# An S4 convolution with a parallel feed-forward block: tiles 0 and 1 loaded and normalised one by one, first weights requested before tiles 2 and 3, the second weight buffer taken into use later

## The chip, the cores and the metric

The kernel runs on one core of one Trainium2 chip. The metric is the device time of one execution in microseconds (us), as the median of several runs. All arithmetic is fp32, or fp32r for the products of TensorE: an operand is split into a high part and the remainder, and three of the four partial products are summed.

## The reference

```python
def reference(A_u, A_A_re, ..., B_x, B_w1, B_w2):
    x = A_u                                   # 1 x 2048 x 576
    xn = layernorm(x)                         # over the 576 columns
    return x + ssm(xn, ...) + ffn(xn, B_w1, B_w2)

def ssm(u, A_re, A_im, B_re, B_im, C_re, C_im, log_dt, Dskip):
    dt = exp(log_dt)                          # 576 channels, 128 states each
    P = exp(dt * A * arange(L))
    K = einsum("dn,dnl,dn->dl", C, P, dt * B).real
    return causal_convolution(u, K) + u * Dskip       # by FFT in the reference

def ffn(x, w1, w2):                           # 576 -> 4608 -> 576
    return silu(x @ w1) @ w2
```

## The kernel before

**Tiling.** The 2048 rows are 16 tiles of 128 rows, handled in pairs. `phase0` takes a pair: it loads it (`load_x`), normalises it (`norm`), transposes each tile on TensorE and splits it into high and low parts (`put_xt`: `xh` by a copy on ScalarE, `xl` by a subtraction on VectorE, and the 64 columns left over in `x4`), and stores the normalised rows to DRAM (`dxn`) for the convolution. Tiles 0 to 3 form block 0 of the feed-forward part and tiles 4 to 7 block 1. Tiles 8 to 15 are transposed in the same way, but their transposes go to DRAM (`dxt`) for the second half.

**The feed-forward part** (`ffn`) runs over two halves of the rows, in each over 36 groups of 128 hidden columns, four groups to a chunk (in the second half, from the third chunk on, in a form with fewer products, `wino_ffn`). For every chunk and block, `up` makes four groups of hidden values (14 products each, into one of two PSUM banks) and the gate (`gf` by SiLU on ScalarE, `gh` a copy, `gl` a subtraction on VectorE). `down` multiplies them with the second weights into `po` and adds the result to `acc` on VectorE. For the very first block, `up` runs in two parts: columns 0 to 255 (tiles 0 and 1) for all four groups, then columns 256 to 511 (tiles 2 and 3).

**Weights.** `load_w1(half, c, t)` loads two groups of first weights at once, as 512, 64 and 64 rows in three DMAs. `split_w1` makes `w1h` (ScalarE, line 266) and `w1l` (VectorE, line 268) of it. There is one raw buffer for them in the pool `wp`; once the pool `w1x` exists, the groups with t = 2 take a second buffer there, and `next_w1` loads a chunk ahead. Second weights are loaded by `load_w2` and split by `split_w2` in the same way (lines 275, 284, 286).

**Beside it** runs `side()`, a generator that `weave` advances at fixed steps of the feed-forward generator: the rest of `phase0`, the parameters of the state-space part (`natural`, whose tables are loaded by SP into memory that the pool `pa` of the first tiles held, lines 652 and 665), the convolution kernel (`kgen`), the spectral product and the tail. The pool `w1x` opens together with `kgen`.

**What sets the order.** The program is written in this woven order. A scheduler then orders the instructions of each engine by its own estimate of time, within the dependences. `tc.issue_after` (in `behind`) keeps instructions behind a named one, `tc.high_priority` moves some ahead. On the chip each engine, and each queue of DMA issues (SP, ScalarE, GpSimd), takes its instructions in that order. The start before is: `side` up to tiles 0 to 3 (`next(sd)`), then the first weights, their splits and the second weights (`next(fg)`), then tiles 4 to 7 (`next(sd)`), then the weave.

Lines that the change and the prediction touch: 118 to 128 (`put_xt`), 161 to 167 (`load_x`), 176 to 197 (`norm`), 199 to 227 (`phase0`, `normed`), 237 to 247 (`load_w1`), 258 to 269 (`split_w1`), 346 to 354 (first loads), 1025 to 1057 (`side`), 1074 to 1079 (start of the program).

Of the kernel before, what the change touches and what calls it, by code (L numbers as in the profile page):

```python
# [41 lines left out]
def kernel(  # L42
# [21 lines left out]
    nc = tc.nc  # L64
    FT = 4
# [44 lines left out]
    acc = {}  # L110
# [4 lines left out]
        x4 = xtp.tile([P, 512], F32R, tag="x4", name=f"x4_{blk}")  # L115
        return xh, xl, x4

    def put_xt(xh, xl, x4, src):

        pt = pss.tile([P, NKT, P], F32, tag="pss", name="pt")  # L120
        for kt in range(NKT):
            nc.tensor.transpose(pt[:, kt, :], src[:, kt * P:(kt + 1) * P], ident)
        nc.scalar.copy(xh, pt)  # L123
        nc.vector.tensor_sub(xl, pt, xh)
        pt = pss.tile([P, 512], F32, tag="pss", name="pt4")
        nc.tensor.transpose(pt[:64, :P], src[:, NKT * P:D], ident)
        pins["xt_s"] = nc.scalar.copy(x4[:64, :], pt[:64, :P]).ins
        pins["xt_v"] = nc.vector.tensor_sub(x4[64:, :], pt[:64, :P], x4[:64, :]).ins
# [32 lines left out]
    def load_x(j, pool, tag, engines):  # L161

        t = pool.tile([P, 2, D], F32, tag=tag, name=f"{tag}{j}")
        for ps, v, eng in quarters(xv, engines):
            eng.dma_start(t[ps], v[:, j:j + 2])
        pairs[j] = t
        return t[:, 0, :], t[:, 1, :]

# [5 lines left out]
    def norm(p0, js, xs):  # L174

        n = len(js)
        st = p0.tile([P, 2, 2, 6], F32, tag="st", name="st")
        mv = p0.tile([P, 2, 2], F32, tag="mv", name="mv")
        for i in range(n):
            for h in range(2):  # L180
                nc.vector.bn_stats(out=st[:, i, h, :], in_=xs[i][:, h * HD:(h + 1) * HD])
            nc.vector.bn_aggr(out=mv[:, i, :], in_=st[:, i, :, :])
        sd = p0.tile([P, 2], F32, tag="sd", name="sd")
        mb = p0.tile([P, 2], F32, tag="mb", name="mb")
        nc.vector.tensor_scalar(sd[:, :n], mv[:, :n, 1], 1e-5, None, op0=ALU.add)
        pins["sd"] = nc.gpsimd.tensor_tensor(sd[:, :n], sd[:, :n], mhalf[:, :n], op=ALU.pow).ins
        xn = p0.tile([P, 2, D], F32, tag="xn", name="xn") if js[0] < 8 else pairs[js[0]]
        for i, j in enumerate(js):
            if j % 2 == 0:
                pins["xn"] = nc.vector.tensor_scalar(xn[:, i, :], xs[i], mv[:, i, 0:1], sd[:, i:i + 1],  # L190
                                                 op0=ALU.subtract, op1=ALU.mult).ins
            else:
                nc.vector.scalar_tensor_tensor(mb[:, i:i + 1], mv[:, i, 0:1], -1.0, sd[:, i:i + 1],
                                               op0=ALU.mult, op1=ALU.mult)
                nc.scalar.activation(xn[:, i, :], xs[i], AF.Identity,
                                     scale=sd[:, i:i + 1], bias=mb[:, i:i + 1])
        return xn

    def phase0(p0, js):
        j0 = js[0]  # L200
        if j0 < 8:
            xs = load_x(j0, accp, "acc", (nc.sync, nc.scalar) if j0 < 4 else (nc.sync,))
            acc.update(zip(js, xs))
        else:
            xs = load_x(j0, p0, "xj", (nc.sync,))
        if j0:
            normed(p0, js, xs)
        else:
            for j, xj in zip(js, xs):
                normed(p0, (j,), (xj,))  # L210

    def normed(p0, js, xs):
        xn = norm(p0, js, xs)
        for i, j in enumerate(js):
            b, jj = divmod(j, 4)
            if b < 2:
                if jj == 0:
                    xts[b] = new_xt(b)
                c = slice(jj * P, (jj + 1) * P)
                xh, xl, x4 = xts[b]  # L220
                put_xt(xh[:, :, c], xl[:, :, c], x4[:, c], xn[:, i, :])
            else:
                xt = p0.tile([P, 9, P], F32R, tag="xt", name="xt", bufs=1)
                put_xt(xt[:, 0:4, :], xt[:, 4:8, :], xt[:, 8, :], xn[:, i, :])
                nc.gpsimd.dma_start(dxt[b - 2][:, :, jj * P:(jj + 1) * P], xt.bitcast(F32))
        eng = nc.sync if js[0] < 8 else nc.gpsimd
        eng.dma_start(dxn[:, js[0]:js[0] + len(js)], xn[:, :len(js)])

    def ffn():
        w2v = w2.rearrange("(t p) d -> p t d", p=P)  # L230
# [6 lines left out]
        def load_w1(half, c, t, pool=None):  # L237

            f = c * FT + t
            first = half == 0 and c == 0  # L240
            r1 = (pool or (pa if first and t else w1x if t and w1x else wp)).tile([P, 5, 2 * P], F32, tag="w1r", name="w1r", bufs=1)
            fs = slice(f * P, (f + 2) * P)
            eng = nc.gpsimd if first and t == 0 else nc.sync
            eng.dma_start(r1[:, 0:4, :], w1[0:512, fs].rearrange("(k p) f -> p k f", p=P))
# [13 lines left out]
        def split_w1(half, c, t):  # L258
            first = half == 0 and c == 0
            r1 = R1.pop((half, c, t))  # L260
            for i in range(2):
                h1 = wp.tile([P, 5, P], F32R, tag="w1h", name="w1h", bufs=FT + 1)
                l1 = wp.tile([P, 5, P], F32R, tag="w1l", name="w1l", bufs=FT + 1)
                src = r1[:, :, i * P:(i + 1) * P]
                with behind(pins.get("gh", pins["xt1s"] if t else None)):
                    nc.scalar.copy(h1, src)
                with behind(pins["xt1"] if first else None):
                    pins["w1l"] = nc.vector.tensor_sub(l1, src, h1).ins
                W1[half, c, t + i] = h1, l1
# [75 lines left out]

        for t in (0, 2):
            load_w1(0, 0, t)
        for t in (0, 2):
            split_w1(0, 0, t)
        for t in range(FT):  # L350
            load_w2(0, 0, t)
        for t in range(FT):
            split_w2(0, 0, t)
        yield 0
# [667 lines left out]
    def side():  # L1022
# [3 lines left out]
        with tc.tile_pool(name="pa", bufs=4) as pa:  # L1026
            for js in ((0, 1), (2, 3), (4, 5), (6, 7)):
                with behind(pins["xt3"] if js[0] > 2 else None):
                    phase0(pa, js)
                pins[f"xt{js[1]}"], pins[f"xt{js[1]}s"] = pins["xt_v"], pins["xt_s"]  # L1030
                if js[0] == 2:
                    yield 0
# [1 line left out]
        with tc.tile_pool(name="kf", bufs=1) as kfp:  # L1034
            for n in ("f", "rho", "phi"):
                kf[n] = kfp.tile([P, D], F32, name=n + "T")
            with tc.tile_pool(name="nat", bufs=1) as nat, tc.tile_pool(name="pb", bufs=2) as pb:
                nt = natural(nat)
                tiles = iter(range(8, NJ, 2))
                for at, tables in ((0.0, 1), (0.02, 0), (0.035, 0), (gate_of(1), 1), (0.06, 0), (gate_of(2), 1), (0.08, 0), (0.085, 1)):  # L1040
# [3 lines left out]
                    else:  # L1044
                        j = next(tiles)
                        with behind(pins["gl"]):
                            phase0(pb, (j, j + 1))
            with behind(pins["sd"]):
                nc.gpsimd.dma_start(f1, cf1)
            nc.sync.dma_start(vt, cv)  # L1050
            with tc.tile_pool(name="up", bufs=1) as up, tc.tile_pool(name="w1x", bufs=1) as w1x:
                sp = spread(up)
                for n, at in enumerate(kgen()):
                    if n > 1:
                        next(sp, None)
                    yield marks[0] + at * (marks[1] - marks[0])
                for _ in sp:
# [13 lines left out]
        yp = ctx.enter_context(tc.tile_pool(name="yp", bufs=3))  # L1071
        yield from tail()

    sd = side()
    next(sd)
    fg = ffn()
    next(fg)
    next(sd)
    weave(fg, 276, sd)
    for j in range(8, 14, 2):  # L1080
        store(pairs[j], j, (nc.sync, nc.scalar))
# [80 lines left out]
```

## Time and profile before

| | us |
|---|---|
| median of 3 runs | 1121.45 |
| lowest and highest | 1119.86, 1123.09 |
| the profiled execution | 1121.59 |
| its span in the trace | 1119.7 |
| TensorE busy | 1091.6 |
| first TensorE instruction | 8.82 |
| first product of the feed-forward part | 12.50 |

The profile is one execution. "L298" is line 298 of the kernel; PE is TensorE's matmul, PEld its weight load, DVE VectorE, ACT ScalarE, POOL GpSimd, SP the engine that issues most DMAs; SPq, ACTq and POOLq are the queues of DMA issues. Matmuls overlap in their pipeline, so the pace of products is read from start to start and not from the length of a row. A window's row gives, for each engine, busy time and number of instructions, then the clock granted to TensorE, the busy share of the DMA engines and GB/s.

### The profile page before, as it was taken

The page shows a single profiled execution, that of the slowest core. Times are in us where ns is not written, and L with a number is a line of the kernel's source. Part 1 is how long each engine was busy: PE and PEld are TensorE (multiplying, and loading weights), DVE is VectorE, ACT ScalarE, POOL GpSimd, SP SyncE. Part 2 cuts the span into 40 slices and gives each one's busy share as a digit, 9 for nine tenths or more (in the row PEclk, how much of TensorE's full clock was granted, in tenths as well). Part 3 has the DMA queues.
Part 4 walks back from the last instruction along what each step waited for, and adds up shares of the span by engine and source line. Part 5 has one row for each costly group of instructions (what it writes and reads, how often), then busy time and mean ns, then how long its engine had stood idle before and what let it go on. Part 6 is the DMA issues. An engine that isn't in the chain of part 4 may idle for free.

```text
span 1119.7 us, 23109 instructions
## 1 busy us (share of the span) xinstructions
PE 1091.6 (97%) x9101; PEld 987.6 (88%) x9101; DVE 950.0 (85%) x1615; ACT 728.1 (65%) x1285; POOL 140.5 (13%) x244
## 2 busy tenths in 40 slices
PE   6998999999999999999999999999999999999998
PEld 5997989889988899898899988899989998999787
DVE  6698899999999999999999978988878888886333
ACT  4665455776777766676667645877767877785330
POOL 1022100000000000000330001112212112111220
PEclk9999999999999999999999999999999999999999
DMA  9455632436353536356964235456455565543985
GB/s 272 141 156 177 194 124 82 144 85 176 105 154 128 150 108 172 120 138 236 237 190 92 72 65 183 133 175 178 140 165 178 163 187 157 167 157 116 247 200 139
DMA packets 161870, 173.68 MB, mean 155 GB/s; under 512 B 88497, under 2 KB 127425, under 8 KB 161121
## 3 DMA queue, kind: packets, MB, share of 16 engines
q1 hardware_dynamic: 137200, 106.75, 34.5%
q0 software_dynamic: 23888, 63.67, 19.2%
q10 hardware_dynamic: 672, 1.77, 0.7%
q8 instruction: 72, 1.18, 0.4%
q14 instruction: 38, 0.30, 0.1%
HBM read 109.64 MB, written 62.60 MB: 154 GB/s over the span
## 4 chain that ended last, share of the span: by engine, by line
PE 70%; DVE 10%; DMA 9%; ACT 5%; issue 4%; SPq 1%; POOL 1%; ACTq 0%; DVEq 0%; POOLq 0%
PE po L328 30%; PE ph L298 16%; PE pb L453 5%; PE kp L866 3%; DMA w<-dw 2%; PE pc L453 2%; DMA w1r<-in_B_w_dram 2%; PE pb L994 2%; PE pu L994 2%; PE pk L994 2%; PE ph L299 1%; PE ph L300 1%; PE z L881 1%; PE pa L453 1%; DMA w2r<-in_B_w_dram 1%
## 5 line engine op out<-in xcount | busy, mean ns | idle before, releaser
L328 PE MATMUL po<-w,gh 128*128 128x288 f32 x2304 | 475.1, 297 | 6.2 <-ACT w L284 2.1
L328 PEld LDWEIGHTS po<-w,gh 128*128 128x128 f32 x2304 | 376.5, 188 | 22.1 <-DMA w<-dw 2.7
L328 PE MATMUL po<-w,gl 128*128 128x288 f32 x1152 | 334.9, 296 | 0.6 <-DVE gl L308 0.6
L328 PEld LDWEIGHTS po<-w,gl 128*128 128x128 f32 x1152 | 215.2, 188 | 2.6 <-DVE gl L308 0.9
L333 DVE TENSOR_TENSOR acc<-po,acc 128x288 f32<-128x288 f32 x296 | 130.3, 452 | 59.7 <-PE po L328 58.6
L298 PE MATMUL ph<-xh,w1h 128*128 128x512 f32 (+1 forms) x368 | 99.1, 388 | 0.9 <-ACT xh L123 0.7
L298 PE MATMUL ph<-xl,w1h 128*128 128x512 f32 (+1 forms) x368 | 98.5, 386 | 0.0
L298 PE MATMUL ph<-xh,w1l 128*128 128x512 f32 (+1 forms) x368 | 97.9, 383 | 0.0
L306 ACT ACTIVATE gf<-ph 128x512 f32<-128x512 f32 (+1 forms) x92 | 53.3, 579 | 60.4 <-PE ph L300 41.8
L298 PEld LDWEIGHTS ph<-xl,w1h 128*128 128x128 f32 x368 | 67.6, 191 | 12.8
L298 PEld LDWEIGHTS ph<-xh,w1l 128*128 128x128 f32 x368 | 66.6, 189 | 11.7
L298 PEld LDWEIGHTS ph<-xh,w1h 128*128 128x128 f32 x368 | 65.2, 191 | 11.2 <-ACT xh L123 1.0
L157 POOL DMA_DIRECT2D d1u<-u x32 | 17.5, 547 | 405.8 <-ACT u L156 404.5
L825 ACT ACTIVATE c<-th,magic 128x1040 f32<-128x1040 f32 x36 | 42.0, 1168 | 40.2 <-DVE C L846 28.0
L307 ACT CAST gh<-gf 128x512 fp32r<-128x512 f32 (+1 forms) x92 | 55.3, 602 | 15.5 <-PE po L328 14.5
L903 POOL DMA_DIRECT2D m<-in_cm_dram x64 | 33.9, 531 | 250.8 <-PE pu L994 147.1
L308 DVE TENSOR_TENSOR gl<-gf,gh 128x512 fp32r<-128x512 f32 (+1 forms) x92 | 60.7, 662 | 3.5 <-ACT gh L307 3.3
L827 ACT ACTIVATE c<-th 128x1040 f32<-128x1040 f32 x36 | 38.7, 1076 | 33.7 <-DVE th L826 33.6
L845 DVE TENSOR_TENSOR S<-th,C 128x1024 f32<-128x1024 f32 x36 | 44.0, 1222 | 12.1 <-ACT th L828 12.0
L470 DVE TENSOR_TENSOR gl<-gf,gh 128x512 fp32r<-128x512 f32 x56 | 38.0, 688 | 11.9 <-ACT gh L469 11.6
L370 ACT CAST w1h<-w1r 128x512 fp32r<-128x512 f32 (+2 forms) x56 | 34.6, 621 | 20.3 <-DMA w1r<-in_B_w_dram 14.6
L826 DVE SCALAR_TENSOR_TENSOR th<-c,th 128x1040 f32<-128x1040 f32 x36 | 44.5, 1237 | 0.7 <-ACT c L825 0.5
(271 smaller groups left out, 2384.5 us busy)
## 6 DMA issues: line engine op xcount, KB each, us to landing
w1r<-in_B_w_dram SPq DMA_DIRECT2D x35, 512.0 KB, 4.2
dw<-w SPq DMA_DIRECT2D x28, 576.0 KB, 4.5
w<-dw POOLq DMA_DIRECT2D x28, 576.0 KB, 6.6
w2r<-in_B_w_dram SPq DMA_DIRECT2D x44, 288.0 KB, 5.0
d1u<-u POOLq DMA_DIRECT2D x32, 288.0 KB, 2.7
d1k<-stage SPq DMA_DIRECT2D x18, 512.0 KB, 7.3
ur<-d1u SPq DMA_DIRECT2D x32, 288.0 KB, 3.3
kr<-d1k SPq DMA_DIRECT2D x32, 288.0 KB, 2.8
```

The source lines that it names most:

```text
L298: nc.tensor.matmul(ph, w[:, kt, :], v[:, kt, a:e], start=n + kt == 0, stop=False)
L306: nc.scalar.activation(gf, ph, AF.Silu)
L307: pins["gh"] = nc.scalar.copy(gh, gf).ins
L308: pins["gl"] = nc.vector.tensor_sub(gl, gf, gh).ins
L328: pins["pe"] = nc.tensor.matmul(po[:, :HD], gs[g][:, js], ws[:, w, hs], start=n == 0 and j not in begun, stop=n == 3 * len(terms) - 1, ski ...
L333: nc.vector.tensor_add(acc[j][:, hs], po[:, :HD], acc[j][:, hs])
L453: pins["pe"] = nc.tensor.matmul(dst, a[:, kt], v[:, kt], start=start and n == 0, stop=stop and n == 5, skip_group_check=True).ins
L825: nc.scalar.activation(c65, th, AF.Identity, bias=magic)
L826: nc.vector.scalar_tensor_tensor(th, c65, MAGIC, th, op0=ALU.subtract, op1=ALU.subtract)
L827: nc.scalar.activation(c65, th, AF.Abs)
L845: nc.vector.tensor_mul(ov3, t[:, :, 0:64].rearrange("n d (x y) -> n d x y", y=32), mv3)
L994: nc.tensor.matmul(dst, st, mv[:, hs], start=n == 0, stop=n == 3 * len(terms) - 1)
```

## The change

- `load_x` loads tiles 0 and 1 as two loads of four DMAs each (72 KB a DMA), first all of tile 0. The pair of tiles 2 and 3, and all later ones, go through SP alone; before, tiles 2 and 3 used SP and ScalarE.
- `phase0` became a generator that stops after the load of tiles 0 to 7. The start steps `side` and `ffn` in turn: load of tiles 0 and 1; first weights' load; tiles 0 and 1 normalised and transposed, load of tiles 2 and 3; second weights' load and first weights' split; tiles 2 and 3; second weights' split; tiles 4 to 7; the weave.
- All first weights are loaded through SP; before, the very first piece went through GpSimd. The normalised rows of tiles 0 to 7 are stored through GpSimd; before, through SP.
- Tile 1 is normalised on VectorE (one `tensor_scalar`), as tile 0 is; before, on ScalarE.
- Tiles 2 and 3 are normalised behind tile 1's last VectorE step. Tile 0's low part waits until both tiles are normalised.
- Of the first four weight copies to `w1h`, the first waits for tile 0's last ScalarE step and the other three for tile 1's; before, the first two waited for no such step.
- The pool `w1x` still opens with `kgen`, but is put to use only from the third step of `kgen`, so the second buffer and the loads a chunk ahead begin later.

Its description also names idle products, products made only to keep TensorE busy: neither the kernel before nor the diff has any.

```diff
-    def put_xt(xh, xl, x4, src):
+    def put_xt(xh, xl, x4, src, low=None):
...
-        nc.vector.tensor_sub(xl, pt, xh)
+        with behind(low):
+            nc.vector.tensor_sub(xl, pt, xh)
...
-        for ps, v, eng in quarters(xv, engines):
-            eng.dma_start(t[ps], v[:, j:j + 2])
+        for i in range(j, j + 2, 1 if j == 0 else 2):
+            for ps, v, eng in quarters(xv, engines):
+                if j == 0:
+                    eng.dma_start(t[ps, i], v[:, i])
+                else:
+                    eng.dma_start(t[ps], v[:, j:j + 2])
...
-            if j % 2 == 0:
+            if j % 2 == 0 or n == 1:
...
     def phase0(p0, js):
         j0 = js[0]
         if j0 < 8:
-            xs = load_x(j0, accp, "acc", (nc.sync, nc.scalar) if j0 < 4 else (nc.sync,))
+            xs = load_x(j0, accp, "acc", (nc.sync, nc.scalar) if j0 == 0 else (nc.sync,))
             acc.update(zip(js, xs))
+            yield
         else:
             xs = load_x(j0, p0, "xj", (nc.sync,))
         if j0:
-            normed(p0, js, xs)
+            with behind(pins["xt1"] if j0 == 2 else None):
+                normed(p0, js, xs)
         else:
-            for j, xj in zip(js, xs):
-                normed(p0, (j,), (xj,))
+            xn = [norm(p0, (j,), (xj,)) for j, xj in zip(js, xs)]
+            last = pins["xn"]
+            for j in js:
+                turned(p0, (j,), xn[j], None if j else last)
+                pins[f"xt{j}s"] = pins["xt_s"]
+
     def normed(p0, js, xs):
-        xn = norm(p0, js, xs)
+        turned(p0, js, norm(p0, js, xs))
+
+    def turned(p0, js, xn, low=None):
...
-        eng = nc.sync if js[0] < 8 else nc.gpsimd
-        eng.dma_start(dxn[:, js[0]:js[0] + len(js)], xn[:, :len(js)])
+        nc.gpsimd.dma_start(dxn[:, js[0]:js[0] + len(js)], xn[:, :len(js)])
...
-            eng = nc.gpsimd if first and t == 0 else nc.sync
+            eng = nc.sync
...
-                with behind(pins.get("gh", pins["xt1s"] if t else None)):
+                with behind(pins.get("gh", pins["xt1s" if t + i else "xt0s"])):
...
         for t in (0, 2):
             load_w1(0, 0, t)
+        yield 0
+        for t in range(FT):
+            load_w2(0, 0, t)
         for t in (0, 2):
             split_w1(0, 0, t)
-        for t in range(FT):
-            load_w2(0, 0, t)
+        yield 0
...
-                    phase0(pa, js)
+                    for _ in phase0(pa, js):
+                        if js[0] <= 2:
+                            yield 0
...
-            with tc.tile_pool(name="up", bufs=1) as up, tc.tile_pool(name="w1x", bufs=1) as w1x:
+            with tc.tile_pool(name="up", bufs=1) as up, tc.tile_pool(name="w1x", bufs=1) as more:
                 sp = spread(up)
                 for n, at in enumerate(kgen()):
                     if n > 1:
+                        w1x = more
                         next(sp, None)
...
-    sd = side()
-    next(sd)
-    fg = ffn()
-    next(fg)
-    next(sd)
+    sd, fg = side(), ffn()
+    for g in (sd, fg, sd, fg, sd, fg, sd):
+        next(g)
     weave(fg, 276, sd)
```

More of the change, by code (lines that the diff above doesn't have):

```diff
@@ L220, in normed @@
                 xh, xl, x4 = xts[b]
-                put_xt(xh[:, :, c], xl[:, :, c], x4[:, c], xn[:, i, :])
+                put_xt(xh[:, :, c], xl[:, :, c], x4[:, c], xn[:, i, :], low)
             else:
@@ L1046, in side @@
                         with behind(pins["gl"]):
-                            phase0(pb, (j, j + 1))
+                            for _ in phase0(pb, (j, j + 1)):
+                                pass
             with behind(pins["sd"]):
```

## The prediction

> **What bounds the kernel now.** I read the page's busy shares, then the table of windows, then the table of waits. Columns of the windows: length, busy time and number of instructions for PE, weight load, VectorE, ScalarE, GpSimd, then granted clock, DMA share, GB/s.
>
> ```profile
> span 1119.7 us, 23109 instructions
> PE 1091.6 (97%) x9101; PEld 987.6 (88%) x9101; DVE 950.0 (85%) x1615; ACT 728.1 (65%) x1285; POOL 140.5 (13%) x244
> ...
> 0.00:12.50 12.50, 2.67 (x11) 1.73 (x11) 5.61 (x22) 4.88 (x9) 4.39 (x11) 1.00 0.89 227
> ...
> 50.00:100.00 50.00, 47.91 (x279) 42.19 (x278) 46.95 (x89) 34.45 (x49) 8.85 (x9) 1.00 0.51 148
> ...
> 400.00:500.00 100.00, 100.00 (x1025) 90.65 (x1015) 97.28 (x147) 69.34 (x105) 4.32 (x8) 1.00 0.43 118
> ```
>
> TensorE sets the time: in the middle it never rests. Only the first 12.5 us (2.67 busy) and the stretch from 50 to 100 (47.91 of 50) leave something to win. The waits say the same:
>
> ```profile
> PE pt L122 <- DVE xn L190: 8.8, 1, 8.8
> PE po L328 <- ACT w L284: 2.1, 1, 2.1
> PE pt L122 <- ACT xj L195: 1.7, 1, 1.7
> ```
>
> All three lie within the first 103 us, where the change works. The amount of products is unchanged, so the new time is the old one minus the idle TensorE time that is really removed. What counts is the lead (how much earlier TensorE stands at the same amount of work) and whether later waits take it back.
>
> **The start.** In order of time, with start, length, engine; a bracket is the idle time before.
>
> ```profile
> 0.74 3.47 DMA acc<-in_A_u_dram
> ...
> 0.74 1.78 SPq L165 DMA_DIRECT2D acc<-in_A_u_dram  x4
> 1.96 0.81 POOL L244 DMA_DIRECT2D w1r<-in_B_w_dram  x1
> 5.66 1.54 DVE L181 BATCH_NORM_STATS2 st<-acc 128x6 f32<-128x288 f32 x4 [4.72 <-DMA acc<-in_A_u_dram]
> 7.11 0.33 DVE L182 BATCH_NORM_AGGREGATE mv<-st 128x2 f32<-128x12 f32 x2
> 7.58 1.22 POOL L186 TENSOR_TENSOR sd<-sd,mhalf 128x1 f32<-128x1 f32 x2 [3.75 <-DVE sd L185]
> 8.18 0.58 DVE L190 TENSOR_SCALAR xn<-acc,mv,sd 128x576 f32<-128x576 f32 x1 [0.55 <-POOL sd L186]
> 8.82 1.12 PE L122 MATMUL pt<-ident,xn 128*128 128x128 f32 x4 [8.82 <-DVE xn L190]
> 9.16 1.54 DVE L181 BATCH_NORM_STATS2 st<-acc 128x6 f32<-128x288 f32 x4 [0.17 <-DMA acc<-in_A_u_dram]
> 10.61 1.35 ACT L266 CAST w1h<-w1r 128x640 fp32r<-128x640 f32 x2
> 11.87 0.58 ACT L123 CAST xh<-pt 128x512 fp32r<-128x512 f32 x1
> 12.35 0.26 ACT L127 CAST x<-pt 64x128 fp32r<-64x128 f32 x1
> 12.50 2.08 PE L298 MATMUL ph<-xh,w1h 128*128 128x256 f32 x8 [0.66 <-ACT xh L123]
> 14.40 3.03 DVE L268 TENSOR_TENSOR w1l<-w1r,w1h 128x640 fp32r<-128x640 f32 x4
> 15.29 2.06 PE L298 MATMUL ph<-xl,w1h 128*128 128x256 f32 x8
> 17.15 0.77 PE L298 MATMUL ph<-xh,w1l 128*128 128x256 f32 x4
> 20.93 0.64 PE L298 MATMUL ph<-xh,w1h 128*128 128x256 f32 x4
> 21.41 0.64 PE L298 MATMUL ph<-xl,w1h 128*128 128x256 f32 x4
> 22.61 0.56 PE L328 MATMUL po<-w,gh 128*128 128x288 f32 x3
> ```
>
> The reader should see a chain, load, statistics, power, normalise, transpose, cast, that ends in the first product at 12.50. Also that eight products from 15.29 to 17.15 take 0.23 each and four from 20.93 take 0.12 each, though the clock column shows 1.00: the first products run at half pace.
>
> **First product.** The whole pair waited for 5.66; its first DMA had landed at 0.74 + 3.47 = 4.21. Tile 0 alone is half the pair and goes first, so I take 4.4. Two statistics (0.77), an aggregate (0.2) and the epsilon (0.2) end at 5.6, the power (0.7) at 6.3. In the changed order tile 1's two statistics stand ahead of tile 0's normalisation on VectorE; tile 1 lands at about 5.7 (as the pair did), so that is free at 6.5 and normalises until 7.1. Transposes at half pace 1.1, to 8.3. ScalarE then does tile 0's casts (0.58 + 0.26, to 9.1), and next in its queue stands the first weight cast, ahead of tile 1's. Tile 1 is normalised at 8.7 on VectorE (ScalarE no longer does it), transposed by 9.85, cast by 10.5. First product 10.5 instead of 12.5: 2.0 gained. The weight cast between them is covered if its load lands by 9.1. It moves from GpSimd's queue to SP's, where it waits for a free DMA slot at about 4.2; the landing row quoted below (3.0/4.9/8.1) gives 9.1 as the middle and 12.3 as the late end. With 12.3, tile 1's cast ends at 13.7 and 1.2 is lost. I take the middle.
>
> **Half of it is given back at tiles 2 and 3.** Before, their statistics ran at 9.16. Now their load stands behind both weight pieces: 0.59 MB for tiles 0 and 1, 0.07 identity, 1.31 weights, 0.59 for tiles 2 and 3 is 2.56 MB, at 0.23 MB/us (first window) 11.1 us after the first packets at 2, so 13.1. VectorE holds these statistics between the second and the third weight subtraction, so the last two (0.76 each) end at 14.7 + 1.5 = 16.3. The first four half groups (56 products) need about 9 us from 10.5, five of them at half pace: 19.4. Tiles 2 and 3 then need, one after the other in ScalarE's order, a normalisation (to 19.7), a gate activation, xh (to 20.7), a gate copy (0.4), x, and xh of tile 3 (0.58): 21.9. Before, all this work of TensorE was behind it at 22.61. The lead is 0.7.
>
> Then the changed order helps: the second four half groups (56 × 0.12 = 6.7) all stand ahead of the second layer's products, so VectorE's statistics of tiles 4 to 7 and the w2 subtractions hide under them. From 21.9 TensorE should run without a wait. Before, it lost another 1.1 until 41 (0.63 of it waiting for gl). Lead at 41: **1.8**. Bounds: 3.2, if ScalarE's chain is not last and work alone sets it; -0.5, if the 0.59 MB of dxn writes, now on GpSimd's queue, get ahead of tiles 2 and 3 (0.59 / 0.23 = 2.5 later).
>
> **The natural loads.**
>
> ```profile
> 40.55 0.27 PE L126 MATMUL pt<-ident,xn 128*64 128x128 f32 x1
> ...
> 40.90 0.33 SPq L665 DMA_DIRECT2D dt<-in_A_log_dt_dram  x1
> 43.16 6.61 DMA cr<-in_A_C_re_dram
> 49.86 0.95 DVE pr L706
> 138.68 0.43 PE L328 MATMUL po<-w,gh 128*128 128x288 f32 x2
> 138.95 0.29 PE L328 MATMUL po<-w,gl 128*128 128x288 f32 x1
> ```
>
> SP's loads of the SSM parameters wait for the last transpose of tile 7, because they reuse its pool. In the changed program 89 second-layer products stand ahead of that transpose, before it was 62: 27 × 0.27 / 2 = 3.6 us more work. So the loads start at 40.9 - 1.8 + 3.6 = 42.7, 1.8 later, and the VectorE chain from 49.86 with them. The queue behind on SP (w2 of the next chunk) moves too, with no use before 70.
>
> **The waits at 94 and 102.**
>
> ```profile
> 86.72 0.59 ACT L123 CAST xt<-pt 128x512 fp32r<-128x512 f32 x1 [6.18 <-DMA dxt<-xt]
> 96.91 0.67 PE L328 MATMUL po<-w,gh 128*128 128x288 f32 x3 [2.09 <-ACT w L284]
> 102.51 0.66 PE L122 MATMUL pt<-ident,xj 128*128 128x128 f32 x4 [1.74 <-ACT xj L195]
> ```
>
> Before, 2.09 + 1.74 and some 0.4 around them are lost, 4.2 in all. In the new order some 6 us more products stand ahead of the fourth w2 tile and of tile 13's transposes, and the fourth w2 load no longer waits behind the third xt cast (the 6.18 row). Both waits should go. Two others come: tile 8's normalisation, 1.8 late on VectorE, against TensorE 1.8 early and with about 2 of slack before (1.6), and the last gate group, whose PSUM bank is freed by an activation that now stands behind the arctangent tables (1.9). Net 4.2 - 3.5 = **0.7** gained. Bounds: 4.2 (none of the new waits) and -1.8 (old waits plus the late loads).
>
> **The second weight buffer.**
>
> ```profile
> DMA to landing us min/median/max: 3.0/4.9/8.1
> ...
> 121.39 0.38 SPq L244 DMA_DIRECT2D w1r<-in_B_w_dram  x1
> 134.63 0.38 SPq L244 DMA_DIRECT2D w1r<-in_B_w_dram  x1
> 140.66 1.20 PE L298 MATMUL ph<-xh,w1h 128*128 128x512 f32 x4 [0.22 <-ACT w1h L266]
> ```
>
> Before, the second half of the third chunk took the extra buffer, whose memory came free late, and TensorE waited 0.4 in all around 140. Now it follows in the one buffer, as soon as the first half is split (119.83 + 1.5 in the old run, by the row order the same place): asked at 121, there at 126, wanted by TensorE 10 us of products earlier than before, at about 127. I take **0.4** gained; the late landing (8.1 instead of 4.9) would cost 3.2 instead. This also bounds what SP's order does to the loads behind it.
>
> Sum: 1.8 + 0.7 + 0.4 = 2.9. The profiled execution took 1121.59 (span 1119.7 and 1.9 around it), 0.14 above the median of the runs shown, so 1121.45 - 2.9 = **1118.6**. The removed ScalarE normalisations, the extra yields, the dxn stores on GpSimd (0.55 each, whose queue idles 3.75 at a time) and the behind-pins cost nothing that I can place: they hide under TensorE, and uncovered the three stores would be 1.7. There are no idle products in the old code to remove.
>
> **The rivals.**
> - *All of it is kept.* The start gives 3.2 and the new waits at 94 to 103 do not come (4.2): 1121.45 - 3.2 - 4.2 + some 0.4 of reordering = 1114. For it: the new order has 6 us more cover there. Against: VectorE is full from 50 to 100 (46.95 of 50).
> - *The lead is given back.* The two new waits were priced with the natural chain 1.8 late. If it comes another 2.5 later (the range of one w1 landing, 4.9 to 8.1, would do it), they grow from 3.5 to 6.0 and eat the 1.8 and the 4.2: 1121. For it: VectorE has no slack to catch up. Against: the old waits hung on ScalarE and a load, not on VectorE.
> - *Slower.* The one buffer for the first weights makes a chain out of split, load and cast. It decides as soon as load and cast need more than the 10 us of products between the two halves of the third chunk. With the late landing the second half costs 3.2, and the next piece, which waits for that split in turn, the same again: 6.4, against the 2.5 gained before: 1121.45 + 3.9 = 1125.4. For it: SP's queue is in order, so what stands ahead delays the load. Against: the fourth chunk is wanted some 40 us later.
> - *The half pace lasts longer.* The start now has gaps between 8 and 11 and again at 20 to 22. If the slow pace holds for 56 more products, 56 × 0.11 = 6.2 less the 3.5 of waits it hides: 1118.6 + 2.7 = 1121.3. [...]
>
> **How the numbers follow.** Forecast 0.40 (its own range 1115 to 1121), all kept 0.22, given back 0.15, slower 0.15, half pace 0.08. A measurement of this kernel can tell about 0.3%, 3.4 us, from no change: under 1118.1 lie all of the second and nearly half of the first, 0.42; over 1124.8 the slower case and a little, 0.17; between, 0.41. The rest of the program is reordered too, which I give 2 us either way. Range 1112 to 1126.
>
> **What would show it.** First product at 10.5 (wrong: after 12). The 256-wide products restart after tile 3's cast near 22. SP's first natural load near 42.7. The waits on w (L284) and on the second xj transpose gone, others of 1 to 2 us near 65 and 100. Wait on w1h near 127 under 1. If the products of the middle no longer run gapless, the whole argument fails.

## The result and the profile after

| | before | after |
|---|---|---|
| median, us | 1120.18 (13 runs) | 1127.63 (13 runs) |
| lowest and highest | 1117.94, 1123.09 | 1122.44, 1131.68 |
| the profiled execution | 1121.59 | 1122.44 |
| its span | 1119.7 | 1120.3 |
| first product | 12.50 | 10.97 |

The ratio of after to before is 1.0062 (95% interval 1.0047 to 1.0077): 7 us slower, where 1118.6 was forecast. One caution for everything that follows: the profiled execution of the changed kernel is the quickest of its 13, 5 us below their median. It shows where time goes, not how much in a usual run; for that the kernel was profiled a second time (experiment 4).

The page of the changed kernel, its span and busy times:

```profile
span 1120.3 us, 23108 instructions
PE 1093.2 (98%) x9101; PEld 986.8 (88%) x9101; DVE 951.6 (85%) x1615; ACT 722.7 (65%) x1284; POOL 140.0 (12%) x246
```

The same three windows as in the prediction, columns as there:

```profile
0.00:12.50 12.50, 4.18 (x17) 3.28 (x18) 5.82 (x18) 5.02 (x10) 3.22 (x9) 1.00 0.83 236
50.00:100.00 50.00, 49.15 (x285) 43.01 (x284) 44.65 (x82) 37.71 (x52) 6.79 (x8) 1.00 0.46 140
400.00:500.00 100.00, 99.37 (x1096) 89.01 (x1095) 98.70 (x143) 71.07 (x109) 4.32 (x8) 1.00 0.39 115
```

The first two windows are better than before (4.18 against 2.67, 49.15 against 47.91). The third, in the middle, no longer is full: 99.37 against 100.00. The table of waits (total, times, longest) says on what:

```profile
PE pt L122 <- DVE xn L195: 7.9, 2, 7.1
PE po L339 <- DVE acc L344: 5.6, 7, 1.8
PE ph L309 <- ACT gf L317: 1.6, 4, 0.9
PE z L894 <- ACT kt L886: 1.4, 1, 1.4
```

The two waits of 2.1 and 1.7 us that the prediction wanted gone are gone. In their place stands `po` waiting for VectorE's additions into `acc` (line 344), which free its PSUM banks: 5.6 us in seven waits. Before, that row was:

```profile
PE po L328 <- DVE acc L333: 1.7, 2, 1.1
```

The start, in order of time:

```profile
3.98 0.82 DVE L186 BATCH_NORM_STATS2 st<-acc 128x6 f32<-128x288 f32 x2 [3.04 <-DMA acc<-in_A_u_dram]
6.82 1.99 SPq L170 DMA_DIRECT2D acc<-in_A_u_dram  x4
8.84 0.73 ACT L277 CAST w1h<-w1r 128x640 fp32r<-128x640 f32 x1
10.97 1.22 PE L309 MATMUL ph<-xh,w1h 128*128 128x256 f32 x4 [0.46 <-ACT xh L123]
13.96 1.54 DVE L186 BATCH_NORM_STATS2 st<-acc 128x6 f32<-128x288 f32 x4 [0.41 <-issue]
19.80 0.60 PE L122 MATMUL pt<-ident,xn 128*128 128x128 f32 x4
20.34 0.60 PE L122 MATMUL pt<-ident,xn 128*128 128x128 f32 x4
20.43 0.58 ACT L123 CAST xh<-pt 128x512 fp32r<-128x512 f32 x1
21.37 0.58 ACT L123 CAST xh<-pt 128x512 fp32r<-128x512 f32 x1
22.01 1.21 PE L309 MATMUL ph<-xh,w1h 128*128 128x256 f32 x8
43.72 0.31 SPq L678 DMA_DIRECT2D dt<-in_A_log_dt_dram  x1
```

The first product comes 1.53 earlier. But the transposes of tiles 2 and 3 now stand behind all first half groups (at 19.80; before, they ran between them, at 14.37 and 17.99), and TensorE has nothing else until ScalarE has cast both: 2.2 us from 19.80 to 22.01, with 1.0 of transposes in them. VectorE has a part in it: the last transpose, at 21.80, had waited 0.86 us for the subtraction `xl` of tile 2.

To compare kernels whose orders differ, I count work. Each product of each trace is given the median interval from its start to the next start that products of its kind and width have in the trace of before. The *delay* at some amount of work is the time at which TensorE gets there, less that work. In us, worked out from the traces:

```
work done, us                          40    100    150    350    550    650   1000
before                               14.7   19.0   20.1   22.4   23.8   24.4   32.9
after                                13.9   17.9   19.3   23.4   29.1   30.3   34.0
after, second profile (exp. 4)       14.7   19.9   21.8   25.9   32.3   33.5   40.5
start of before, mean of 6 profiles  14.9   18.1   19.4   21.8   25.1   27.0   35.2
new start, mean of 7 profiles        14.7   18.9   22.2   25.0   28.8   30.3   38.1
```

(The six: before and experiments 1, 3, 6, 8, 11. The seven: after and experiments 2, 4, 5, 7, 10, 12.) Work 40 is reached at about 55 us, work 650 near 680. In the profile of after the lead is 0.8 at 40, has turned into a lag of 5.9 by 650 (before has a stall of 1.3 close to that point, so the figure can be about 1 less), and 4.8 of that comes back by 1000, because before loses some stalls between 650 and 950 that after does not have. The windows show the same, first of before, then of after:

```profile
0.00:150.00 150.00, 135.49 (x848) 123.04 (x849) 122.75 (x252) 84.97 (x141) 23.80 (x32) 1.00 0.64 192
150.00:650.00 500.00, 498.55 (x5085) 449.61 (x5084) 477.47 (x704) 339.95 (x506) 37.36 (x72) 1.00 0.48 136
650.00:1000.00 350.00, 343.71 (x2269) 315.52 (x2269) 297.89 (x560) 262.46 (x553) 60.64 (x113) 1.00 0.55 160
```

```profile
0.00:150.00 150.00, 137.77 (x853) 124.46 (x854) 118.82 (x243) 81.58 (x140) 23.35 (x34) 1.00 0.59 180
150.00:650.00 500.00, 493.70 (x5046) 442.59 (x5045) 477.58 (x705) 337.58 (x504) 37.35 (x72) 1.00 0.48 139
650.00:1000.00 350.00, 347.47 (x2308) 320.69 (x2307) 303.40 (x569) 261.80 (x553) 60.60 (x113) 1.00 0.55 161
```

TensorE is 2.3 us busier up to 150, 4.9 us less from 150 to 650. And the column to look at is the third, VectorE: at 150 us it has done 118.82 of work, 3.9 less than before, and from there it is over 95% busy in both kernels (477.5 of 500).

### The profile page after: what moved, and what is told of

Same layout as the page of the kernel before. It is cut to its first block, busy times and chain, and to the rows that moved or that the text cites. A ratio compares the mean times of both kernels' runs of the same rounds, so it can differ in the third digit from the quotient of the medians.

```text
span 1120.3 us, 23108 instructions
## 1 busy us (share of the span) xinstructions
PE 1093.2 (98%) x9101; PEld 986.8 (88%) x9101; DVE 951.6 (85%) x1615; ACT 722.7 (65%) x1284; POOL 140.0 (12%) x246
## 4 chain that ended last, share of the span: by engine, by line
PE 61%; DVE 19%; issue 8%; DMA 6%; ACT 5%; POOL 1%; SPq 0%; ACTq 0%; DVEq 0%; POOLq 0%
PE po L339 27%; PE ph L309 11%; PE pb L466 5%; PE pc L466 2%; DMA w<-dw 2%; PE pb L1007 2%; PE kp L879 2%; DVE acc L344 2%; PE pk L1007 2%; PE pu L1007 2%; DMA w2r<-in_B_w_dram 2%; DVE th L822 1%; PE pa L466 1%; DVE th L839 1%; DVE gl L319 1%
```

## The experiments

### 1 and 2: the two parts of the change, each alone

Experiment 1 is the kernel before with the later second weight buffer:

```diff
-            ... tc.tile_pool(name="w1x", bufs=1) as w1x:
+            ... tc.tile_pool(name="w1x", bufs=1) as more:
...
                     if n > 1:
+                        w1x = more
                         next(sp, None)
```

> The kernel before with one part of the change alone: the second buffer of first weights is taken from the third kernel piece on instead of from the opening of its pool; the start is that of before. Theory A (the buffer costs the time: from 140 us on the middle runs with fewer weights asked for ahead, and the products wait): 1125 to 1128 us, and the lost time between 150 and 650 us grows as in the changed kernel, about 10 us more than before at 650. Theory B (the new start costs it: the loads and splits in another order push VectorE's work into the middle): 1119 to 1121 us, no change. Theory C (neither by itself: every change moves the order that the scheduler makes of the whole middle, and some orders leave VectorE's additions behind kernel pieces): anywhere from 1117 to 1127, with the products stopped on the additions into acc at other places than in the changed kernel.

Measured 1120.87, ratio 1.001 (0.9993 to 1.0027). The later buffer alone costs nothing that can be told; theory A falls.

Experiment 2 is the changed kernel with that edit undone, the new start alone.

> The changed kernel with the second buffer of first weights open as early as before: the new start alone. Theory A (buffer): 1117 to 1119 us, the 2 us of the earlier first product and nothing lost in the middle. Theory B (start): 1126 to 1129 us, as the changed kernel. Theory C (order of the middle): anywhere from 1116 to 1128; the lead at 100 us is 2 to 3 us in any case, and what is left at 650 us differs from the changed kernel's -10.

Measured 1127.62, ratio 1.007 (1.0045 to 1.0094). The slowdown goes with the new start. But its trace loses the time at another place. Its waits between 125 and 150 us, then SP's queue and a row of TensorE there:

```profile
PE ph L309 <- ACT w1h L277: 6.5, 1, 6.5
```

```profile
129.80 0.43 SPq L286 DMA_DIRECT2D w2r<-in_B_w_dram  x1
139.55 0.66 PE L674 MATMUL ptk<-ident,t 96*128 96x96 f32 x6
139.83 0.33 SPq L299 DMA_DIRECT2D dw<-w  x1
140.33 1.02 SPq L255 DMA_DIRECT2D w1r<-in_B_w_dram  x1
```

The load of the first weights into the extra buffer is asked for at 140.33; before, it was asked for at 134.63. That buffer lies in memory that held the state-space parameters, and in the kernel before the waits of SP's queue name what frees it, the last transposes of these parameters (`ptk`):

```profile
SPq L244 <- PE ptk L661: 3.6, 1, 3.6
133.90 0.66 PE L661 MATMUL ptk<-ident,t 96*128 96x96 f32 x6
```

In both traces the load leaves 0.1 us behind the end of these transposes, 134.56 and 140.21. VectorE had made their input at 128.77 before and at 132.85 here. The store of a split second weight (line 299) stands ahead of the load in the queue, but left at 139.83 and was not the last to be ready. TensorE stands 6.5 us. In the changed kernel the same piece comes through the one buffer, asked for at 129.32, whatever the parameters do, and there is no such wait. So the later buffer saves this stop, yet the time is the same: from work 150 to 650 experiment 2 loses 3.2 us (29.4 to 32.6), the changed kernel 11.0 (19.3 to 30.3). While TensorE stands, VectorE goes on (from 140 to 150 us it is busy 7.1, TensorE 3.5); what is lost in one piece here is lost in small ones there.

### 3 and 4: another order with the same start, and the changed kernel again

```diff
-        marks = (0.1357, 0.613, 0.855)
+        marks = (0.1375, 0.613, 0.855)
```

> The kernel before with nothing of the change: only the point from which the kernel pieces are woven in moves by half a step of 276 (first mark 0.1357 to 0.1375). The work, the buffers and the start are the same; the scheduler's order of the middle is another. Theories A and B: 1119 to 1121.5 us, since neither the buffer nor the start is touched. Theory C (the order of the middle is worth some microseconds either way): at least 2 us from 1120.2, up or down, with the difference arising between 150 and 650 us.

Measured 1130.67, ratio 1.0097 (1.0073 to 1.0121): the largest slowdown so far, by an edit that adds and removes no work and leaves the first 90 us as they were. Half of what theory C said holds: an order alone is worth 10 us. The place does not: the delay at 650 is 24.1, as before; the time is lost behind it, 7 us between work 650 and 700 alone, above all in one wait of 4.9 us near 691:

```profile
ACT kh L985 <- DMA kr<-d1k: 8.2, 3, 5.2
PE po L328 <- ACT gh L469: 4.9, 1, 4.9
```

`po` waits for the gate on ScalarE, and ScalarE stands at a piece of the convolution kernel (`kr`) whose load, asked for at 685.88, took 7.8 us to land; the median of that load is 2.8 in the kernel before. The stall costs more than its length: the granted clock is 0.93, 0.50 and 0.89 in the windows of 5 us from 690, which at 0.50 is 6.8 us (694.3 to 701.1), and 0.93 and 0.73 in those from 830, 3.4 us more from 834 on; up to 5 us of the 10 in all.

> The changed kernel once more, for the profile of another execution: its profiled one took 1122.4, its median 1127.6. All theories: 1126 to 1129 in the median. If the spread of its executions comes from waits in the middle (theory C), this profile shows more lost time between 150 and 650 us than the first, on the additions into acc; if it comes from the start's transfers (theory B), it shows a later restart of the products between 19 and 42 us.

Measured 1129.28, ratio 1.0082 (1.0058 to 1.0105); profiled execution 1128.65. The stalls of the first profile are all there again, at the same work (the third line of the table runs parallel to the second from 150 to 550): in these two profiles the stalls of the middle belong to the program, not to the execution. What differs is the start (restart at 22.77 instead of 22.01), the clock after one stall, and stalls from 650 on (7.0 against 3.7 of delay up to 1000). The windows around 110 us, clock in the third column from the end:

```profile
105.00:110.00 5.00, 3.20 (x24) 2.81 (x23) 4.97 (x13) 0.27 (x1) 0.96 (x1) 1.00 0.90 323
110.00:115.00 5.00, 5.00 (x28) 5.00 (x28) 4.89 (x11) 1.34 (x3) 2.27 (x4) 0.66 0.64 229
```

The 0.66 is a mean over 5 us, with 1.00 in the windows on both sides. At 0.50, the lowest clock of any window of these runs inside the program (experiment 3, 695 to 700), it stands for 3.4 us of the five.

The stall itself is in every profile of the new start with its VectorE work whole. In the first profile of after:

```profile
104.74 1.54 DVE L186 BATCH_NORM_STATS2 st<-xj 128x6 f32<-128x288 f32 x4
106.20 0.93 DVE L749 TENSOR_TENSOR aim<-t,aim 96x768 f32<-96x768 f32 x1
107.06 0.75 DVE L716 SCALAR_TENSOR_TENSOR ex<-ex,r 128x576 f32<-128x576 f32 x1
107.84 0.40 DVE L344 TENSOR_TENSOR acc<-po,acc 128x288 f32<-128x288 f32 x1
108.28 0.76 DVE L344 TENSOR_TENSOR acc<-po,acc 128x288 f32<-128x288 f32 x2
108.29 0.53 PE L339 MATMUL po<-w,gh 128*128 128x288 f32 x2 [1.80 <-DVE acc L344]
```

No DVE row has an idle bracket: VectorE works without a break on statistics and on the state-space parameters, and the addition that frees TensorE's bank is in the queue behind them. This is the new wait, 1.8 us, and nobody is late but VectorE.

### 5 to 8, 10 to 12: pairs at equal marks

The first mark was set to 0.1339, 0.1375, 0.1393 and 0.1430 in both kernels (the line of experiment 3), so that each start is seen in five orders.

> The changed kernel with the first mark at 0.1375: the partner of the third experiment, which had the start of before (1130.7 us). Theory D (the new start is worth its 2 us, and the order that the scheduler makes of everything behind it is a draw that swamps them): the pair differs from the pair at 0.1357 (1120.4 and 1128.3); here anything from 1117 to 1130, and lower than 1130.7 is likely. Theory B (the new start itself costs 7 us behind 100 us): about 1137 us.

> The kernel before with the first mark at 0.1339, half a step of 276 earlier. Theory D: another draw, 1117 to 1131 us; the start up to 90 us is that of before to 0.5 us. Theory E (the mark of before is simply the right one for its start, and a later point costs, an earlier one gains or costs nothing): 1117 to 1121 us.

> The changed kernel with the first mark at 0.1339, about as much earlier as its products start earlier. Theory D: 1117 to 1130 us, and on the mean over the marks the changed kernel lies 0 to 3 us below the kernel before at the same mark. Theory E (the kernel pieces must keep their distance from the start): 1117 to 1119 us, the predicted gain. Theory B: 7 us above the kernel before at this mark.

> The kernel before with the first mark at 0.1393, a whole step later. Theory D: another draw, 1117 to 1131 us. Theory E (later costs): more than the 1130.7 us of half a step.

> The changed kernel with the first mark at 0.1393, the partner of the eighth experiment (1122.6 us with the start of before). Theory D: 1119 to 1131, and the four differences at equal marks (so far +7.9, -4.0, +5.2) keep both signs or come near nothing. Theory B: 1127 to 1130.

> The kernel before with the first mark at 0.1430, two steps later: one more draw of the order with the start of before. Theory D: 1117 to 1131. Theory B: 1120 to 1123, with the 1130.7 at 0.1375 an exception.

> The changed kernel with the first mark at 0.1430. Theory D: 1117 to 1131, on either side of the kernel before at the same mark. Theory B: 1126 to 1130.

| first mark | start of before, us (interval of the ratio) | new start, us (interval of the ratio) | difference, us |
|---|---|---|---|
| 0.1339 | 1123.05 (0.9995 to 1.0032) | 1128.28 (1.0047 to 1.0094) | +5.2 |
| 0.1357 | 1120.18 and 1120.38 | 1127.63 and 1129.28 | +7.4 and +8.9 |
| 0.1375 | 1130.67 (1.0073 to 1.0121) | 1126.63 (1.0029 to 1.0067) | -4.0 |
| 0.1393 | 1122.55 (1.0003 to 1.0038) | 1133.34 (1.0088 to 1.0130) | +10.8 |
| 0.1430 | 1120.25 (0.9974 to 1.0001) | 1130.40 (1.0053 to 1.0111) | +10.2 |

Theory E falls (later marks do not simply cost). Of B and D neither holds as written. The order is a draw worth up to 10 us, as D says; but the new start lies above at four marks of five. The mean difference is 6 us (with 8.2 for the second row), its 95% interval from the scatter of the five -1.4 to 13.5: the pairs lean to a cost of the start and do not settle it.

The windows from 150 to 650 us say a little more. TensorE's idle time there (500 less its busy time) is larger with the new start at every mark: in the order of the table 6.1 against 4.7, 6.3 and 7.2 against 1.5, 5.9 against 1.6, 3.1 against 2.4, 5.5 against 2.1. The mean difference is 3.0 us (0.7 to 5.4 by the same reckoning), half of the 6. Two profiles stand across it: 5.1 idle in experiment 1, with the start of before (profiled in the slowest of its 12 executions, 1126.25), and 0.5 in experiment 2, with the new one.

### 9: why the lead of the start is lost

Tiles 2 and 3 are asked for right behind tiles 0 and 1, ahead of the weights:

```diff
+    early = {}
...
-            xs = load_x(j0, accp, "acc", (nc.sync, nc.scalar) if j0 == 0 else (nc.sync,))
+            xs = early.pop(j0, None) or load_x(j0, accp, "acc", (nc.sync, nc.scalar) if j0 == 0 else (nc.sync,))
+            if j0 == 0:
+                early[2] = load_x(2, accp, "acc", (nc.sync,))
```

> The changed kernel with the load of tiles 2 and 3 put back ahead of the weights in SP's queue. Theory F (the lead of the start is lost because this pair lands late: its statistics began at 13.96 us in one execution and at 15.61 in another, and the second half groups restarted at 22.01 and 23.44): statistics by 11 us, first product near 11.5 to 12 because the weights come later, restart by 22 in every execution, and the lead over the kernel before at 40 us of product work, 0 on the mean of five profiles, becomes 0.7 to 1. Theory G (the lead is lost because both transposes stand behind the first half groups on TensorE, and their casts follow one after the other): restart 2.2 us after the last first half group whatever the load does, lead 0 or less. For the whole time theory D leaves 1117 to 1130 us; theory B (the start as such costs 7 us) leaves 1126 to 1129.

Measured 1128.72, ratio 1.0079 (1.0058 to 1.0099). The start in its trace:

```profile
12.69 1.23 PE L312 MATMUL ph<-xh,w1h 128*128 128x256 f32 x4 [2.08 <-ACT xh L123]
14.45 1.53 DVE L187 BATCH_NORM_STATS2 st<-acc 128x6 f32<-128x288 f32 x4
21.79 0.60 PE L122 MATMUL pt<-ident,xn 128*128 128x128 f32 x4
24.01 1.22 PE L312 MATMUL ph<-xh,w1h 128*128 128x256 f32 x8
```

Theory G: with the load early, the restart is again 2.2 us behind the end of the first half groups (24.01 less 21.79), as in the profile of after (22.01 less 19.80). All that the edit did is to move the weights, and with them the first product, 1.7 us back. The statistics did not come earlier, 14.45 against 13.96, because VectorE has them behind the first weight subtraction; so theory F's condition, statistics by 11 us, never came about, and the run does not test it. A late landing of the pair can add to the 2.2: in experiment 7 its statistics began at 15.61 and the restart was at 23.44.

### 13 to 16: VectorE relieved

Two small VectorE operations of each kernel piece are left out, in both kernels and at two marks:

```diff
-                with behind(pins["gl"]):
-                    nc.vector.tensor_add(split(th)[:, :, :, :32], split(th)[:, :, :, :32], col(phiT, i, 32))
...
-                    nc.vector.scalar_tensor_tensor(dst[:, :, 32:64], ...)
+                    if dst is S:
+                        nc.vector.scalar_tensor_tensor(dst[:, :, 32:64], ...)
```

> The kernel before without two of VectorE's small operations in each kernel piece (the addition of phi to the angles, and the last product of the cosine table): 72 instructions of 0.69 us, some 48 us of the 478 that VectorE is busy between 150 and 650 us, are left out, nothing else. Theory D (the middle loses time because VectorE is nearly full and the order of its queue decides which product waits): the time lost by TensorE between 150 and 650 us falls from 4 to 10 us to under 3, and the whole time to 1110 to 1117 us. Theory B (the new start costs it): about as before, 1118 to 1121.

> The changed kernel with the same two operations left out. Theory D: within 3 us of the run before with VectorE relieved, at 1110 to 1118. Theory B: still 6 to 8 us above it.

> The kernel before with the first mark at 0.1393 and the same two operations left out. Theory D: within 3 us of the same at the mark of before. Theory B: the same as with the full VectorE (1122.6) less at most 2.

> The changed kernel with the first mark at 0.1393 and the same two operations left out; with a full VectorE this pair was 10.8 us apart, the widest. Theory D: within 3 us of its partner. Theory B: 6 to 11 above.

| first mark | start of before, us (interval of the ratio) | new start, us (interval of the ratio) | difference, us |
|---|---|---|---|
| 0.1357 | 1114.41 (0.9930 to 0.9962) | 1116.71 (0.9959 to 0.9983) | +2.3 |
| 0.1393 | 1114.32 (0.9935 to 0.9971) | 1118.76 (0.9964 to 0.9994) | +4.4 |

The middle of the two at 0.1357, start of before first:

```profile
150.00:650.00 500.00, 499.31 (x5216) 450.11 (x5216) 445.49 (x641) 337.35 (x505) 38.27 (x73) 1.00 0.50 138
```

```profile
150.00:650.00 500.00, 498.94 (x5213) 449.43 (x5212) 453.67 (x654) 341.74 (x511) 38.28 (x73) 1.00 0.50 142
```

With VectorE at 89 to 91% instead of 95.5, TensorE is busy 498.94 of 500 with the new start, 5.2 more than with the full VectorE. The kernels with the start of before gain 6 and 8 us, those with the new start 12 and 15, and the pairs come together, from 8 and 11 apart to 2 and 4. At 0.1357 the gain lies where theory D puts it, in the middle. What stays there is of the start itself: the stall at 108 us, which lies ahead of the relief, in this profile with a slow clock behind it (0.95 from 105 to 110 us, 0.71 from 110 to 115; delay at work 100: 20.0 against 17.4, as much as the 2.3).

At 0.1393 the gain lies elsewhere. From 150 to 650 TensorE with the new start is busy 496.88 in experiment 10 and 496.55 with the relief, and still waits 2.2 for additions into `acc`; the 15 us come behind 650, where experiment 10 had the stall of experiment 3 (`po` waiting 3.8 us for the gate, behind a load of `kr`) and a clock of 0.99, 0.50 and 0.83 in the windows of 5 us from 690, 0.99 and 0.67 from 830 and 0.66 from 905, 13.6 us if all of it was at 0.50. The 4.4 that stay are more than theory D's 3 and less than theory B's 6. Leaving out work also makes the scheduler draw a new order, and these two marks had two of the three widest gaps, so a new draw alone would be likely to narrow them. That a full VectorE carries the difference is supported by the first pair and not by the second.

### 17 and 18: a debt put on, a debt taken off

```diff
         for i in range(0, NT, 2):
+            v.reciprocal(t1[:, i:i + 2], t0[:, i:i + 2])
             v.reciprocal(t0[:, i:i + 2], t0[:, i:i + 2])
```

> The kernel before with three more reciprocals, 4.96 us of VectorE work near 66 us whose results are overwritten. Theory H (the new start hands VectorE a debt: its work done stands 1.8 us lower at 75 us and 4.2 us lower at 150 us than with the start of before, in every profile, and a queue 95% full does not pay it back): a debt of 5 us put on by hand costs the same kind of time, 1124 to 1128 us. If VectorE still has room for it: 1119 to 1121.5.

Measured 1128.3, ratio 1.0061 (1.0039 to 1.0083). The time is the one that theory H named, but not by its way. The windows of its trace:

```profile
125.00:150.00 25.00, 17.33 (x121) 16.10 (x120) 18.76 (x33) 11.40 (x20) 2.48 (x3) 0.88 0.70 216
150.00:650.00 500.00, 499.24 (x5068) 449.18 (x5067) 474.87 (x700) 337.19 (x506) 37.12 (x72) 1.00 0.49 137
```

then the wait in it, the transposes and SP's queue:

```profile
PE ph L298 <- ACT w1h L266: 6.8, 1, 6.8
139.04 0.66 PE L661 MATMUL ptk<-ident,t 96*128 96x96 f32 x6
139.42 0.33 SPq L288 DMA_DIRECT2D dw<-w  x1
139.91 1.08 SPq L244 DMA_DIRECT2D w1r<-in_B_w_dram  x1
```

It is the stop of experiment 2, in a kernel with the start of before. VectorE makes the parameters' last step at 132.49 instead of 128.77, the transposes that free the extra buffer end at 139.70 instead of 134.56, and the load of the weights is asked for at 139.91 instead of 134.63. So work put on VectorE reached TensorE by way of a buffer that came free late; the middle, where theory H has the loss, loses nothing. For theory H's own path this run does not count.

```diff
-        for i in range(0, NT, 2):
-            v.reciprocal(t0[:, i:i + 2], t0[:, i:i + 2])
```

> The changed kernel without its three reciprocals (the tangents' ratio is then wrong, the work behind it is the same), 4.96 us of VectorE work less near 70 us. Theory H: most of the loss goes, 1120 to 1124 us. If the debt of VectorE at the start of the middle does not matter and only its order does: 1126 to 1130, another draw.

Measured 1121.57, ratio 1.0007 (0.9990 to 1.0024), 6 us below the changed kernel. Its middle:

```profile
150.00:650.00 500.00, 498.91 (x5189) 450.20 (x5191) 477.61 (x705) 338.16 (x502) 37.38 (x72) 1.00 0.49 139
```

VectorE is as busy as in the changed kernel (477.61 against 477.58), but TensorE stands 1.1 us instead of 6.3, and the delay is 21.9 at work 650 instead of 30.3. This is what theory H says; being one order among many, it supports it and does not prove it. It also shows that a full VectorE alone does not stop TensorE: here, before and in experiment 2 VectorE is busy 475 to 478 of the 500 us, and TensorE idles 0.5 to 1.5.

## Why the prediction was wrong

Step by step:

- **First product at 10.5, 2.0 gained.** Measured 10.97; right in its chain, 0.5 too early.
- **Restart near 22.** 22.01 in the profile, 22.6 to 23.4 in the other six profiles of the new start. The chain (transposes behind the half groups, casts one after the other) was right. Its end was read as one more step, while it costs the lead: 2.2 to 2.7 us in the seven profiles of the new start. (A small slip in its sums: 14.7 + 1.5 is 16.2, not 16.3.)
- **Lead of 1.8 at 41 us.** Measured 0.8 in the profile and 0.2 on the mean of seven profiles against six. The term was mis-sized by 1.0 to 1.6: the 1.1 that before loses up to 41 was counted as won, but the new order loses 0.5 of it too, and the restart is mostly later than 22.
- **Natural loads at 42.7.** Measured 43.72; right in direction, 1.0 too early. The prediction moved "the VectorE chain from 49.86 with them" and priced only the wait that it saw at its end. But these loads are the head of VectorE's work, and that is where the debt starts: from 50 to 75 us VectorE is busy 22.13 instead of 24.94, at 75 us it has done 54.51 us of work instead of 56.41, at 150 us 118.82 instead of 122.75.
- **Waits at 94 to 103: 4.2 go, 3.5 come.** The old two went, as said (the first of them was read from one execution: 2.1 there, 0.3 to 1.7 in the other five profiles of the old start). New stalls came, of 0.4 to 0.9 at 78, for a gate on ScalarE (forecast 1.6 at 65, for tile 8), and 1.8 at 108 (forecast 1.9 near 100, behind the arctangent tables; in fact behind VectorE's queue). From work 60 to 100 the new start loses 4.1 on the mean, the old one 3.1: -1.0 instead of +0.7.
- **Second buffer, 0.4.** Nothing that can be told (experiment 1); no wait near 127.
- **"The rest of the program is reordered too, which I give 2 us either way."** This is the step that failed. With the start untouched, four other orders gave -0.1, +2.2, +2.7 and +10.3 us. And the condition that the prediction put on itself, that the products of the middle stay gapless, broke: TensorE's 498.55 of 500 became 493.70; 3.2 of the 6.3 idle are waits for additions into `acc`, the rest mostly waits for ScalarE. I had quoted VectorE's 97.28 of 100 in the middle and read it as cover for TensorE, not as a second bound without room: the lag of its chain was followed to 103 us and then dropped.

Of the rivals, "the lead is given back" named the cause that the runs point to, that VectorE has no slack to catch up, but let the matter end at 103 us. The slower rival named the one buffer for first weights; experiment 1 rules that out, and experiments 2 and 17 show the extra buffer to be the one that came late. The half pace did not last longer: products stood 0.21 apart up to 15.40 and 0.12 from 15.71 on, while before they stood 0.21 apart up to 17.36 and 0.12 from 17.63 on. The forecast also started from 1121.45, the median of three runs; of thirteen it is 1120.18, which hid 1.3 us of the miss.

**What stays open.** That a full VectorE carries most of the loss is supported by the middle of experiments 13 and 14 and not shown: at the other mark the gain lies behind 650. That it is the debt of the start, and not only an unlucky order, rests on four pairs of five, on TensorE's idle time in the middle, on the VectorE work done at 150 us (117.1 to 118.8 in six of the seven profiles of the new start, 120.1 in experiment 2, whose TensorE had stopped by then, and 121.4 to 124.7 in the six of the old) and on experiment 18; the scatter of the orders is too wide to prove it. No kernel with the whole work done beat the kernel before by more than can be told; the nearest is experiment 11.

## What to carry to other kernels

Where TensorE is gapless and VectorE is over 95% busy beside it, as in the middle here (477.5 of 500 us), follow both: a change to the start must be priced by what it leaves undone on VectorE, too. A gain of 2 us cannot be forecast for a program whose order a scheduler draws anew with every edit; look first, with a neutral edit, how far that draw reaches (here 10 us), and compare variants over several draws. An earlier first product is worth only what the next rendezvous, here tiles 2 and 3, lets through: of 1.53 us 0.8 was left at work 40.

## What was not expected of the hardware

The clock. A stall of 1.8 us of TensorE was followed by some 3.4 us at a granted clock of 0.50 in some executions and not in others. The stall of 1.80 at 107 us in experiment 4 was (1.00 from 105 to 110, 0.66 from 110 to 115), the same stall, 1.80, in the first profile of after was not (1.00 in both); of the ten profiles with this stall four were (besides experiment 4 experiment 2 with 0.93 and 0.72, experiment 9 with 1.00 and 0.66, experiment 14 with 0.95 and 0.71), and their delay at work 100 is 19.7 to 20.7, against 17.9 to 18.8 in the six others: about 1.7 us more, half of 3.4 (the 20.7 is experiment 9's, and has its later start in it). This is one source of the changed kernel's wider spread. What decides whether the clock falls was not shown. A price for a stall of 1.8 us has to reach from 1.8 to 3.5 us, an estimate from these ten profiles: 1.8 alone, or with the 1.7 behind it.
